# Queries in rows of four tokens: a new order of q, of the head pairs and of the factors in a retention and feed-forward kernel

## The chip, the cores and the metric

The kernel runs on one core of one Trainium2 chip. The metric is device time in microseconds. Of three runs of the kernel before, the median is 296.56 us (296.47 to 297.73). A profiled execution of its own gave the trace that is read here.

## The reference

Inputs are q, k and v of shape [8 batches, 8 heads, 576 tokens, 64], and two weights, w_in [512, 2048] and w_out [2048, 512], all fp32. Each head h has a decay gamma_h = 1 - 2^(-5-h):

```python
scores = scale * np.matmul(q, k.transpose(0, 1, 3, 2))        # scale = 1/8
Dmat = np.where(rel >= 0, gamma[:, None, None] ** rel, 0.0)   # rel = position of query - of key
ret = np.matmul(scores * Dmat, v)
x = ret.transpose(0, 2, 1, 3).reshape(4608, 512)
h = x @ w_in
g = h * np.tanh(softplus(h))
out = g @ w_out                                               # [4608, 512] fp32
```

## The kernel before

**Tiling.** The 4608 tokens are 36 chunks of 128. Chunks 0 to 7 are the first 128 tokens of each batch and have a code of their own at the start. Then come, for each pair of batches, chunks 1, 2 and 3 of either batch and one tail chunk (c = 4) that holds the last 64 tokens of both: 28 chunks, 24 of them whole (c < 4) and 4 tails. Four chunks make a tile t of 512 tokens; there are nine tiles.

**The dense part.** For a tile, `g1` (L579) multiplies w_in by xT, the transposed retention output, into a PSUM bank `hp` of 512 columns, and ScalarE (ACT) applies the activation (L590). `g2` (L595) multiplies by w_out into a bank `ops`; `store` (L640) copies it out and SyncE (SP) sends it to memory. All matmuls of both go through `product` (L551), which issues one of 512 columns (L553) or two of 256 (L558). There are two `hp` banks and one `ops` bank.

**The retention part.** The decay is split into a factor on the query and a factor on key and value: q is scaled by gamma^position, v by gamma^-position, and a causal mask of 64 by 64 is all that is left between them; keys stay unscaled. A running state (a sum of k times v over all earlier tokens of a batch) carries the rest. For chunk n the steps are:

- `load` (L298): on POOL's DMA queue, q, k and v of the chunk into `qkraw` and `vraw`, token by token, in pieces of 64 floats. Tiles `qkraw` have five buffers, `vraw` seven. Loads 12 and 13 are paced by hand: each waits for the landing of the sixth DMA before it (`paced`, L292).
- `step_p` (L322): on VectorE (DVE), two multiplications (L330) turn `qkraw` into `qks` in bf16, q with its factor `gq` and k with ones, and put the heads in pairs.
- `step_v` (L333): v times its factor, on DVE up to chunk 19 and on GpSimd (POOL) from chunk 20.
- `step_t` (L342): the eight 128x128 blocks of `qks` are transposed to `qkT`, up to chunk 13 on TensorE (PE, L351) with a copy by ACT, from chunk 14 by a DMA of SP (L359).
- `visit` (L524), once for every two chunks, 14 in all. It puts the attention matmuls of 64 by 64 on PE: the new states (`states`, L428), the outputs of the masked scores (`outputs`, L487), the queries times the state (`outputs_end`, L504), and the next two chunks' scores (`step_s`, L373). `outputs_copy` (L516) then copies the two banks of outputs, one by ACT and one by DVE, into `xT`, and `step_m` (L379) applies the mask.

The order of the work on each engine is written out by hand: loops over units of dense work call the steps at fixed units (L753 and L800), and every engine and queue works in that order. Each load on POOL's queue waits for the landing of the eighth DMA before it.

**The start.** DVE makes positions (`pos`, L135), distances (L151 to L153), the decay mask `dmask` (L156) and an identity (L158), then `ex` (L661, eight operations of 128x5) from which ACT makes the factors `gq` and `gv` (L662, L663), and casts the first q (L665). TensorE keeps warm with zeros (L170, L173), transposes the first chunks (L203) and makes their scores (L222) and outputs (L254).

Of the kernel before, what the change touches and what calls it, by code (L numbers as in the profile page):

```python
# [16 lines left out]
def kernel(  # L17
# [117 lines left out]
        nc.vector.memset(pos[:, c:c + 1], float(P * c))  # L135
    nc.vector.memset(pos[64:P, 4:5], 512.0 - 64.0)
    minus_p = consts.tile([P, 1], F32)
    late = consts.tile([P, P], F32)
    for i in (1, 0):
        for b in (2, 3):  # L140
# [6 lines left out]
    for f0 in (512, 768):  # L147
        load_w_in(f0, 256)
    mask = consts.tile([P, 64], F32)
    lg = [math.log(1.0 - 2.0 ** (-5.0 - h)) for h in range(H)]  # L150
    nc.vector.tensor_copy(minus_p, dist[:, 0:1])  # L151
    nc.vector.tensor_scalar(late, dist, 0.0, 1.0e6, op0=OP.is_lt, op1=OP.mult)
    nc.vector.tensor_tensor(dist, dist, late, op=OP.max)  # L153
# [3 lines left out]
    ex = consts.tile([P, 5, H], F32)  # L157
    nc.vector.tensor_scalar(ident, dist, 0.0, None, op0=OP.is_equal)  # L158

    nc.vector.tensor_scalar(pos, pos, minus_p, None, op0=OP.subtract)  # L160
# [126 lines left out]

    issued = []  # L290

    def paced(ins, n):  # L292

        if N0 + 3 < n < N0 + 6:
            behind(ins, issued[-6])
        issued.append(ins)

    def load(n, gate=None):  # L298
        if n >= n_chunks:
            return  # L300
        b, c = chunks[n]
        qkr = io.tile([P, 2, H, D], F32, name="qkraw")
        vr = io.tile([P, H, D], F32, name="vraw", bufs=7)
        live[n] = {"qkr": qkr, "v": vr}
        for t, src in ((qkr[:, 0], q), (qkr[:, 1], k), (vr, v)):
            if c < 4:
                ins = nc.gpsimd.dma_start(  # L307
                    out=t, in_=src[b, :, ds(P * c, P), :].rearrange("h p d -> p h d"))
                paced(ins, n)
                if gate is not None:  # L310
                    behind(ins, gate)
                    gate = None
            else:
                for e in range(2):
                    ins = nc.gpsimd.dma_start(
                        out=t[ds(64 * e, 64)],
                        in_=src[b + e, :, ds(512, 64), :].rearrange("h p d -> p h d"))
                    if gate is not None:
                        behind(ins, gate)
                        gate = None  # L320

    def step_p(n):  # L322
        c = chunks[n][1]
        qks = io.tile([P, 2, H, D], BF16, name="qks", bufs=4)
        live[n]["qks"] = qks
        slots = qks.rearrange("p i (g x y) d -> p (i g) y x d", x=2, y=2)
        heads = live[n]["qkr"].rearrange("p i (g y x) d -> p (i g) y x d", x=2, y=2)
        factors = gqk[:, c].rearrange("p i (g y x) -> p (i g) y x", x=2, y=2)
# [13 lines left out]
    def step_t(n, gate=None):  # L342
# [66 lines left out]
    def states(n):  # L409

        if n >= n_chunks:
            return [], 0
        st = ps_sc.tile([P, 2, 2, NP, 64], F32, name="sc")
        whole = [b for b, c in chunks[n:n + 2] if c == 1]
        s0 = ps_st.tile([P, 2, NP, 64], F32, name="st")[:, 0] if whole else None

        made = []

        def part(x, j, p):
            r = ds(64 * j, 64)  # L420
            for e in range(2):
                hh = 4 * (p // 2) + 2 * e + p % 2
# [12 lines left out]
        def unit(i, seen=None):  # L435
            made.clear()
            for p in range(NP):
                part(first_half[i], 0, p)
                part(second_half[i], 1, p)
            if seen is not None:  # L440
                behind(made[0], seen)
            return made[-4:]

        def sum_up():
            new = tr.tile([P, 5, NP, 64], F32, name="total", bufs=2)
            lows = tr.tile([P, 5, NP, 64], BF16, name="ssb", bufs=2)
# [32 lines left out]
    def outputs(n, banks):  # L479

        both = [pool.tile([P, NP, 2, 64], F32, name=name) for pool, name in banks]
        for x in range(2):
            vs = live[n + x]["vs"]
            for h in range(NP):
                for j in range(2):
                    for a in range(2):
                        nc.tensor.matmul(both[j][ds(64 * a, 64), h, x, :], lhsT=vs[ds(64 * j, 64), 2 * h + a, :],  # L487
                                         rhs=live[n]["sm"][ds(64 * j, 64), h % 2, x, 2 * (h // 2) + a, :],
                                         start=(x == 0 and h == 0), stop=False, skip_group_check=True)
        return both  # L490

    def outputs_end(n, both, other, seen=None):

        made = []
        for x in range(2):
            b, c = chunks[n + x]
            qk = live[n + x]["qk"]
            for g in range(2):
                for e in range(2):
                    j = e ^ other  # L500
                    state = st_sb[b, c, j] if c < 4 else st_sb[b + j, 4]
                    for a in range(2):
                        r, p = ds(64 * e, 64), 2 * g + a
                        made.append(nc.tensor.matmul(  # L504
                            both[j][ds(64 * a, 64), 2 * g + e, x, :], lhsT=state[r, p, :],
                            rhs=qk[r, 0, p, ds(64 * j, 64)], start=False, stop=True, skip_group_check=True))
# [4 lines left out]
    def outputs_copy(n, both, copies):  # L511
# [1 line left out]
        if s == 0:  # L513
            xts[t] = xp.tile([P, KC, NCH * P], BF16, name="xT")
        for j, copy in enumerate(copies):
            copy(xts[t][:, :, ds(P * s, 2 * P)].rearrange("p h (x j i) -> p j h x i", x=2, j=2)[:, j], both[j])  # L516

    held = consts.tile([P, 2], BF16)

# [137 lines left out]


    nc.scalar.activation(dmask, dmask, AX.Exp, bias=lnd[:, 0:1])
    for h in range(H):  # L660
        nc.vector.tensor_scalar(ex[:, :, h], pos, lg[h], None, op0=OP.mult)  # L661
    nc.scalar.activation(gq, ex, AX.Exp)  # L662
    nc.scalar.activation(gv, ex, AX.Exp, scale=-1.0)  # L663
    for b in range(2):
        dve(fst[0]["qb"][:, b, :], q0[:, b, :])  # L665
# [35 lines left out]
    nc.gpsimd.memset(mask, 1.0)  # L701
    for j in range(2):
        half = mask[ds(64 * j, 64)]
        nc.gpsimd.affine_select(out=half, in_=half, compare_op=OP.is_ge, fill=0.0,
                                base=0, pattern=[[1, 64]], channel_multiplier=-1)
    for b in range(4):
        load(N0 + b)
    nc.vector.tensor_scalar(gq, gq, 1.0 / math.sqrt(D), None, op0=OP.mult)
# [189 lines left out]
```

## Time and profile before

| | us |
|---|---|
| median of three runs | 296.56 (296.47 to 297.73) |
| the profiled execution's own time | 296.89 |
| its span, from the first to the last instruction | 295.2 |
| DVE, multiplications of q and k (L330) | 36.9 in 56 operations of 710 ns |
| POOL, issues of q's loads (L307) | 21.5 in 24 of 895 ns |
| PE, scores (L373), 448 matmuls 64x64x64 | 6.7 |
| copies of outputs to xT (L516), DVE and ACT | 9.0 (13 of 691 ns) and 8.2 (14 of 586 ns; one more stands by itself) |

How to read it: the first rows of the profile give each engine's busy time and its share of the span. The slices cut the span in 40 equal pieces; a digit is the busy share in tenths. The chain follows the work that ended last back from the end, and tells which engine held it up at each step. The timeline gives start, duration, engine, line, output and inputs of each instruction, "xN" for N merged ones, and in brackets how long the engine had been idle and for whom. The list of waits adds up who waited for whom. "L330" is line 330 of the kernel.

### The profile page before, as it was taken

To read this page: it belongs to the slowest core of one execution; us is meant where nothing else is said; L and a number is where in the kernel's file an instruction comes from. 1 tells how busy PE (TensorE), PEld (TensorE's weight loads), DVE (VectorE), ACT (ScalarE), POOL (GpSimd) and SP (SyncE) were. 2 spreads that over 40 slices of the span, in tenths; PEclk is the share of its full clock that TensorE was granted. 3 is DMA by queue.
4 is the path that set the end of the run, shared out by engine and by line. 5 is a ranking of instruction groups with operands and counts; after the bars stand their busy time and mean duration, and the time that the engine had idled before them with its cause. 6 is when DMAs were issued, how large, how long until landed. Compare 5 with 4: busy or idle time off the path is not lost.

```text
span 295.2 us, 7937 instructions
## 1 busy us (share of the span) xinstructions
PE 289.8 (98%) x3486; PEld 159.5 (54%) x3486; DVE 140.7 (48%) x252; ACT 128.2 (43%) x210; POOL 124.8 (42%) x163
## 2 busy tenths in 40 slices
PE   8999999999999999999999999999999999999995
PEld 5566887555557454547545454545454544444443
DVE  5861647589954829454645454535453321000011
ACT  4856226776545534443444434343435333333200
POOL 8845655487157295645576737292020000000000
PEclk9999999999999999999999999999999999999999
DMA  7999999999999999998979889686323111011122
GB/s 155 223 202 205 205 240 231 336 207 204 235 207 223 206 164 236 209 199 171 223 188 210 205 191 223 137 202 145 71 63 75 38 38 67 7 36 50 59 71 71
DMA packets 44067, 47.45 MB, mean 161 GB/s; under 512 B 25984, under 2 KB 33152, under 8 KB 44032
## 3 DMA queue, kind: packets, MB, share of 16 engines
q0 software_dynamic: 15120, 31.20, 50.5%
q1 hardware_dynamic: 28768, 15.54, 24.2%
q8 instruction: 27, 0.44, 0.6%
q10 hardware_dynamic: 144, 0.20, 0.2%
q14 instruction: 8, 0.07, 0.1%
HBM read 37.75 MB, written 9.44 MB: 160 GB/s over the span
## 4 chain that ended last, share of the span: by engine, by line
PE 94%; DMA 3%; POOL 2%; DVE 0%; issue 0%; POOLq 0%
PE hp L553 42%; PE ops L553 31%; PE hp L558 6%; PE ops L558 4%; DMA gT<-in_v_dram 3%; PE sc L373 1%; PE sc L428 1%; PE hp L504 1%; PE hp L487 1%; PE hp L634 1%; POOL gT L107 1%; PE st L558 1%; PE st L428 1%; PE sc L351 1%; PE sc L200 1%; POOL gT L118 0%
## 5 line engine op out<-in xcount | busy, mean ns | idle before, releaser
L553 PE MATMUL hp<-xT,w_in_t 128*128 128x512 bf16 (+1 forms) x524 | 128.2, 376 | 0.0
L590 ACT ACTIVATE gT<-hp 128x512 bf16<-128x512 f32 x142 | 84.7, 597 | 95.2 <-PE hp L553 94.2
L553 PE MATMUL ops<-w_out_t,gT 128*128 128x512 bf16 x416 | 102.6, 379 | 0.0
L553 PEld LDWEIGHTS <-w_in_t 128*128 128x128 bf16 x527 | 51.3, 98 | 53.9 <-issue 0.4
L553 PEld LDWEIGHTS <-gT 128*128 128x128 bf16 x470 | 44.7, 98 | 51.3
L642 DVE COPY res<-ops 128x512 f32<-128x512 f32 x28 | 19.3, 690 | 85.2 <-PE ops L553 85.2
L330 DVE TENSOR_TENSOR qks<-qkraw,gqk 128x512 bf16<-128x512 f32 x56 | 36.9, 710 | 3.6 <-DMA qkraw<-in_k_dram 3.3
L307 POOL DMA_DIRECT2D qkraw<-in_q_dram x24 | 21.5, 895 | 20.8 <-DVE qks L330 7.8
L516 DVE CAST xT<-hp 128x512 bf16<-128x512 f32 x13 | 9.0, 691 | 30.4 <-PE hp L504 30.4
L337 POOL TENSOR_TENSOR vs<-vraw,gv 128x512 bf16<-128x512 f32 x16 | 16.8, 1072 | 15.7 <-PE hp L487 15.6
L307 POOL DMA_DIRECT2D qkraw<-in_k_dram x24 | 21.3, 889 | 3.3 <-DMA vpair<-in_v_dram 1.5
L307 POOL DMA_DIRECT2D vraw<-in_v_dram x24 | 21.2, 884 | 1.8 <-DMA w_out_t<-in_moe_w_out_dram 1.0
L516 ACT CAST xT<-hp 128x512 bf16<-128x512 f32 x14 | 8.2, 586 | 28.6 <-PE hp L504 28.6
L558 PEld LDWEIGHTS <-gT 128*128 128x128 bf16 x180 | 17.3, 98 | 3.7
L522 POOL COPY held<-qkT 128x1 bf16<-128x1 bf16 x8 | 1.5, 187 | 37.7 <-DMA qkT<-qks 37.7
L464 DVE TENSOR_TENSOR total<-sc,total 128x256 f32<-128x256 f32 x40 | 16.9, 422 | 1.0
L379 DVE TENSOR_TENSOR sm<-sc,mask 128x1024 bf16<-128x1024 f32 x14 | 17.0, 1215 | 0.7 <-PE sc L373 0.7
L558 PE MATMUL hp<-xT,w_in_t 128*128 128x256 bf16 x104 | 15.9, 272 | 0.0
L558 PEld LDWEIGHTS <-w_in_t 128*128 128x128 bf16 x106 | 10.4, 98 | 6.6 <-issue 0.2
L467 ACT CAST ssb<-total 128x768 bf16<-128x768 f32 (+3 forms) x13 | 11.6, 895 | 3.3 <-DVE total L464 3.2
L553 PE MATMUL hp<-w_out_t,gT 128*128 128x512 bf16 x52 | 12.7, 379 | 0.0
L558 PE MATMUL ops<-w_out_t,gT 128*128 128x256 bf16 x96 | 12.4, 273 | 0.0
(134 smaller groups left out, 244.9 us busy)
## 6 DMA issues: line engine op xcount, KB each, us to landing
out_dram<-res SPq DMA_DIRECT2D x31, 256.0 KB, 3.6
qkraw<-in_q_dram POOLq DMA_DIRECT2D x24, 256.0 KB, 6.0
qkraw<-in_k_dram POOLq DMA_DIRECT2D x24, 256.0 KB, 6.4
vraw<-in_v_dram POOLq DMA_DIRECT2D x24, 256.0 KB, 6.7
w_out_t<-in_moe_w_out_dram POOLq DMA_DIRECT2D x4, 512.0 KB, 12.0
gT<-in_k_dram POOLq DMA_DIRECT2D x8, 128.0 KB, 6.5
gT<-in_v_dram POOLq DMA_DIRECT2D x2, 512.0 KB, 7.3
w_in_t<-in_moe_w_in_dram POOLq DMA_DIRECT2D x2, 512.0 KB, 10.9
```

Source lines behind the costliest of these rows:

```text
L307: ins = nc.gpsimd.dma_start(out=t, in_=src[b, :, ds(P * c, P), :].rearrange("h p d -> p h d"))
L330: nc.vector.tensor_tensor(slots[:, :, y], heads[:, :, y], factors[:, :, y].unsqueeze(3).to_broadcast([P, NP, 2, D]), op=OP.mult)
L337: engine.tensor_tensor(vs, live[n]["v"], gv[:, c, :].unsqueeze(2).to_broadcast([P, H, D]), op=OP.mult)
L379: nc.vector.tensor_tensor(sm.rearrange("p e x n i -> p (e x n) i"), live[n]["sc"].rearrange("p e x n i -> p (e x n) i"), mask.unsqueeze(1) ...
L428: ins = nc.tensor.matmul(to, lhsT=ks, rhs=vs, start=(x is not None or j == 0 and p == 0), stop=True, skip_group_check=True)
L464: nc.vector.tensor_tensor(new[:, k], st[:, j, x], total[b], op=OP.add)
L467: casts.append(lambda copy: copy(lows[:, 0:k], new[:, 0:k]))
L516: copy(xts[t][:, :, ds(P * s, 2 * P)].rearrange("p h (x j i) -> p j h x i", x=2, j=2)[:, j], both[j])
L553: newest[0] = nc.tensor.matmul(to, lhsT=w, rhs=x, start=first, stop=last)
L558: nc.tensor.matmul(to[:, ts(j, n)], lhsT=w, rhs=x[:, ts(j, n)], start=False, stop=False, skip_group_check=True)
L590: done = nc.scalar.activation(gts[t][:, f, :], hp, AX.Mish)
L642: copy(ot, ops)
```

## The change

For the 24 whole chunks, q is loaded in rows of four consecutive tokens (1 KB): partition 32p + g holds tokens 4g to 4g + 3 of a head, heads 0 to 3 in one DMA and 4 to 7 in a second. After the transposes the queries of a chunk so lie in the order (r, head, g), where the token is 4g + r; `queries` picks the 64 of a head and a half chunk as four runs of 16. Scores, mask and outputs keep that order of queries, and `outputs_copy` puts the tokens back in order as it writes `xT`. The four tail chunks load q as before and are read with steps of four columns. Heads are paired as h and h + 4 instead of within groups of four, in `qks`, in the states and in the outputs. The factors of q become a table `gq` by (r, half of the heads) with the positions of the new order, set up with 36 small memsets and seven operations; k gets no factor and is copied with a cast. The pacing of loads 12 and 13 goes.

```diff
+    lgs = consts.tile([P, H], F32)
+    for h in range(H):
+        nc.vector.memset(lgs[:, h:h + 1], lg[h])
+    lgp = consts.tile([P, 2], F32)
+    quarter = consts.tile([P, 1], F32)
+    for p in range(NP):
+        rows = ds(32 * p, 32)
+        nc.vector.memset(quarter[rows], -128.0 * p)
+        for x in range(2):
+            nc.vector.memset(lgp[rows, x:x + 1], lg[4 * x + p])
+    starts = consts.tile([P, 4, 4], F32)
+    for c in range(4):
+        for r in range(4):
+            nc.vector.memset(starts[:, c, r:r + 1], float(P * c + r))
...
+    nc.vector.tensor_scalar(group, minus_p, -4.0, quarter, op0=OP.mult, op1=OP.add)
+    nc.vector.tensor_scalar(posq, starts, group, None, op0=OP.add)
...
-    gqk = consts.tile([P, 5, 2, H], F32)
-    nc.vector.memset(gqk, 1.0)
-    gq = gqk[:, :, 0, :]
+    gq = consts.tile([P, 5, 4, 2], F32)
+    for x in range(2):
+        nc.vector.tensor_scalar(gq[:, 0:4, :, x], posq, lgp[:, x:x + 1], None, op0=OP.mult)
...
-        if N0 + 3 < n < N0 + 6:
-            behind(ins, issued[-6])
...
+        if c < 4:
+            for x in range(2):
+                moves.append((qr[:, ds(4 * x, 4), :], q[b, ds(4 * x, 4), ds(P * c, P), :].rearrange(
+                    "h (g r) d -> h g (r d)", r=4)))
...
-        for y in range(2):
-            nc.vector.tensor_tensor(slots[:, :, y], heads[:, :, y],
-                                    factors[:, :, y].unsqueeze(3).to_broadcast([P, NP, 2, D]), op=OP.mult)
+        if c < 4:
+            nc.vector.tensor_tensor(
+                qks[:, 0].rearrange("p (r x) d -> p r x d", x=2),
+                live[n]["qr"].rearrange("p (x r) d -> p r x d", r=4),
+                gq[:, c].unsqueeze(3).to_broadcast([P, 4, 2, D]), op=OP.mult)
...
+        nc.vector.tensor_copy(qks[:, 1].rearrange("p (n x) d -> p n x d", x=2),
+                              live[n]["kr"].rearrange("p (x n) d -> p n x d", x=2))
...
+    def queries(n, e, p, j):
+
+        qT = live[n]["qk"][ds(64 * e, 64), 0]
+        if chunks[n][1] == 4:
+            return qT[:, p, ds(64 * j, 64)].rearrange("d (g r) -> d r g", r=4)
+        return qT.rearrange("d r (p j g) -> d r p j g", j=2, g=16)[:, :, p, j, :]
...
-                        nc.tensor.matmul(sc[i, e, x, p, :], lhsT=qk[r, 1, p, i], rhs=qk[r, 0, p, i],
+                        nc.tensor.matmul(sc[i, e, x, p, :], lhsT=qk[r, 1, p, i], rhs=queries(n + x, e, p, j),
...
-                            both[j][ds(64 * a, 64), 2 * g + e, x, :], lhsT=state[r, p, :],
-                            rhs=qk[r, 0, p, ds(64 * j, 64)], start=False, stop=True, skip_group_check=True))
+                            both[j][ds(64 * a, 64), 2 * e + g, x, :], lhsT=state[r, p, :],
+                            rhs=queries(n + x, e, p, j), start=False, stop=True, skip_group_check=True))
...
-            copy(xts[t][:, :, ds(P * s, 2 * P)].rearrange("p h (x j i) -> p j h x i", x=2, j=2)[:, j], both[j])
+            copy(xts[t][:, :, ds(P * s, 2 * P)].rearrange("p h (x j g r) -> p j h x r g", x=2, j=2, r=4)[:, j],
+                 both[j].rearrange("p h x (r g) -> p h x r g", r=4))
...
-    for h in range(H):
-        nc.vector.tensor_scalar(ex[:, :, h], pos, lg[h], None, op0=OP.mult)
-    nc.scalar.activation(gq, ex, AX.Exp)
+    nc.vector.tensor_tensor(ex, pos.unsqueeze(2).to_broadcast([P, 5, H]),
+                            lgs.unsqueeze(1).to_broadcast([P, 5, H]), op=OP.mult)
+    nc.vector.tensor_copy(gq[:, 4].rearrange("p r x -> p (r x)"), ex[:, 4, :])
+    nc.scalar.activation(gq, gq, AX.Exp)
...
-                                base=0, pattern=[[1, 64]], channel_multiplier=-1)
+                                base=0, pattern=[[1, 4], [4, 16]], channel_multiplier=-1)
```

More of the change, by code (lines that the diff above doesn't have):

```diff
@@ L137 @@
     minus_p = consts.tile([P, 1], F32)
+    lg = [math.log(1.0 - 2.0 ** (-5.0 - h)) for h in range(H)]
+    lgs = consts.tile([P, H], F32)
[12 more added lines that the diff above has]
+            nc.vector.memset(starts[:, c, r:r + 1], float(P * c + r))
     late = consts.tile([P, P], F32)
@@ L149 @@
     mask = consts.tile([P, 64], F32)
-    lg = [math.log(1.0 - 2.0 ** (-5.0 - h)) for h in range(H)]
     nc.vector.tensor_copy(minus_p, dist[:, 0:1])
@@ L158 @@
     nc.vector.tensor_scalar(ident, dist, 0.0, None, op0=OP.is_equal)
+    group = consts.tile([P, 1], F32)
+    nc.vector.tensor_scalar(group, minus_p, -4.0, quarter, op0=OP.mult, op1=OP.add)
+    posq = consts.tile([P, 4, 4], F32)
+    nc.vector.tensor_scalar(posq, starts, group, None, op0=OP.add)
     nc.vector.tensor_scalar(pos, pos, minus_p, None, op0=OP.subtract)
-    gqk = consts.tile([P, 5, 2, H], F32)
-    nc.vector.memset(gqk, 1.0)
-    gq = gqk[:, :, 0, :]
+    gq = consts.tile([P, 5, 4, 2], F32)
+    for x in range(2):
+        nc.vector.tensor_scalar(gq[:, 0:4, :, x], posq, lgp[:, x:x + 1], None, op0=OP.mult)
     gv = consts.tile([P, 5, H], F32)
@@ L286, in cast_k0 @@
         nc.vector.tensor_tensor(k0[b], k0r[b], gv[:, 0, :].unsqueeze(2).to_broadcast([P, H, D]), op=OP.mult)
-    issued = []
-    def paced(ins, n):
-        if N0 + 3 < n < N0 + 6:
-            behind(ins, issued[-6])
-        issued.append(ins)
     def load(n, gate=None):
@@ L301, in load @@
         b, c = chunks[n]
-        qkr = io.tile([P, 2, H, D], F32, name="qkraw")
+        qr = io.tile([P, H, D], F32, name="qraw")
+        kr = io.tile([P, H, D], F32, name="kraw")
         vr = io.tile([P, H, D], F32, name="vraw", bufs=7)
-        live[n] = {"qkr": qkr, "v": vr}
-        for t, src in ((qkr[:, 0], q), (qkr[:, 1], k), (vr, v)):
-            if c < 4:
[L307 to L312, printed above, removed]
+        live[n] = {"qr": qr, "kr": kr, "v": vr}
+        moves = []
+        if c < 4:
+            for x in range(2):
+                moves.append((qr[:, ds(4 * x, 4), :], q[b, ds(4 * x, 4), ds(P * c, P), :].rearrange(
+                    "h (g r) d -> h g (r d)", r=4)))
+        for t, src in ((qr, q), (kr, k), (vr, v))[c < 4:]:
+            if c < 4:
+                moves.append((t, src[b, :, ds(P * c, P), :].rearrange("h p d -> p h d")))
             else:
                 for e in range(2):
[L315 to L320, printed above, removed]
+                    moves.append((t[ds(64 * e, 64)], src[b + e, :, ds(512, 64), :].rearrange("h p d -> p h d")))
+        for to, src in moves:
+            ins = nc.gpsimd.dma_start(out=to, in_=src)
+            if gate is not None:
+                behind(ins, gate)
+                gate = None
     def step_p(n):
@@ L325, in step_p @@
         live[n]["qks"] = qks
-        slots = qks.rearrange("p i (g x y) d -> p (i g) y x d", x=2, y=2)
-        heads = live[n]["qkr"].rearrange("p i (g y x) d -> p (i g) y x d", x=2, y=2)
-        factors = gqk[:, c].rearrange("p i (g y x) -> p (i g) y x", x=2, y=2)
-        for y in range(2):
-            nc.vector.tensor_tensor(slots[:, :, y], heads[:, :, y],
-                                    factors[:, :, y].unsqueeze(3).to_broadcast([P, NP, 2, D]), op=OP.mult)
+        if c < 4:
[3 more added lines that the diff above has]
+                gq[:, c].unsqueeze(3).to_broadcast([P, 4, 2, D]), op=OP.mult)
+        else:
+            nc.vector.tensor_tensor(
+                qks[:, 0].rearrange("p (n x) d -> p n x d", x=2),
+                live[n]["qr"].rearrange("p (x n) d -> p n x d", x=2),
+                gq[:, c].rearrange("p r x -> p (r x)").rearrange("p (x n) -> p n x", x=2).unsqueeze(3)
+                .to_broadcast([P, NP, 2, D]), op=OP.mult)
+        nc.vector.tensor_copy(qks[:, 1].rearrange("p (n x) d -> p n x d", x=2),
+                              live[n]["kr"].rearrange("p (x n) d -> p n x d", x=2))
     def step_v(n):
@@ L421, in part @@
             for e in range(2):
-                hh = 4 * (p // 2) + 2 * e + p % 2
+                hh = 4 * e + p
                 if x is None:
@@ L487, in outputs @@
                         nc.tensor.matmul(both[j][ds(64 * a, 64), h, x, :], lhsT=vs[ds(64 * j, 64), 2 * h + a, :],
-                                         rhs=live[n]["sm"][ds(64 * j, 64), h % 2, x, 2 * (h // 2) + a, :],
+                                         rhs=live[n]["sm"][ds(64 * j, 64), h // 2, x, 2 * (h % 2) + a, :],
                                          start=(x == 0 and h == 0), stop=False, skip_group_check=True)
@@ L496, in outputs_end @@
             b, c = chunks[n + x]
-            qk = live[n + x]["qk"]
             for g in range(2):
@@ L703 @@
         half = mask[ds(64 * j, 64)]
-        nc.gpsimd.affine_select(out=half, in_=half, compare_op=OP.is_ge, fill=0.0,
-                                base=0, pattern=[[1, 64]], channel_multiplier=-1)
+        nc.gpsimd.affine_select(out=half.rearrange("p (r g) -> p r g", r=4), in_=half.rearrange("p (r g) -> p r g", r=4), compare_op=OP.is_ge, fill=0.0,
+                                base=0, pattern=[[1, 4], [4, 16]], channel_multiplier=-1)
     for b in range(4):
```

## The prediction

> **What bounds the kernel now.** I read the page's busy times and slices first, then its chain, then the chain and the timeline in narrow windows. The page:
>
> ```profile
> PE 289.8 (98%) x3486; PEld 159.5 (54%) x3486; DVE 140.7 (48%) x252; ACT 128.2 (43%) x210; POOL 124.8 (42%) x163
> ...
> PE   8999999999999999999999999999999999999995
> ...
> PEclk9999999999999999999999999999999999999999
> DMA  7999999999999999998979889686323111011122
> ...
> PE 94%; DMA 3%; POOL 2%; DVE 0%; issue 0%; POOLq 0%
> ```
>
> TensorE is busy in every slice at the full granted clock and is 94% of the chain; DVE, ACT and POOL are under half busy. The DMA engines are full for the first half, yet only 3% of the chain is DMA. That 3% lies at the start (chain of the first 17 us):
>
> ```profile
> 6.14 8.11 DMA gT<-in_v_dram
> 14.26 0.02 issue
> 14.28 0.71 DVE vb L236 x2
> ...
> 15.56 0.98 PE hp L565 x8
> ```
>
> The first values land at 14.26, are cast, and the dense matmuls run from 15.56 to the end. From there the chain is PE pieces one behind the other: 256-column matmuls at 109 ns (chain: 14 in 1.53 us, L558), nowhere an idle row over a few hundred ns. So the time is a start of 15.5 us, set by DMA, and a gapless PE stream. A change gains only by shortening one of the two, and loses wherever it opens a hole in the stream.
>
> **Part 1: q's loads (L307, 24 chunks).** Removed: one DMA of 256 KB in pieces of 256 B, 895 ns to issue on POOL. Added: two of 128 KB in rows of 1 KB. The nearest issue rows are L107 (128 rows each, 530 to 566 ns) and L315 (half a chunk, 694 ns): 1.1 to 1.4 us for the two, so POOL pays 0.2 to 0.5 us more a chunk, 5 to 12 us in all on an engine busy 124.8 of 295.2 us. Cover: in the DMA-bound stretch (34 to 48 us run at about 208 GB/s, one 256 KB load per 1.25 us) POOL waits for landings anyway, since each load waits for the landing of the eighth DMA before it (the list of waits: POOL qkraw <- DMA vpair 3.4 us, though vpair has nothing to do with qkraw). Later POOL idles by several us between visits (POOL held <- DMA qkT 37.7 us in all). Two slots of eight per q instead of one leave two chunks in flight instead of 2.7, still over 6 us of transfers.
>
> The transfer itself: between no gain and the page's best slice (336 GB/s, 0.78 us instead of 1.25), 0 to 0.47 us a chunk. I take half; it is worth nothing at the end, as no PE row waits for it. The pacing that goes (loads 12 and 13 wait for the sixth DMA before; one POOL wait of 2.9 us) lets these loads start earlier: also nothing on PE.
>
> **Part 2: the factors (L330, 28 chunks).** Two DVE multiplies of 128x512 fp32 to bf16, 0.60 us start to start, 1.28 us a chunk, become one multiply (0.68) and one plain cast of k. The same cast stands in L236 (DVE, 128x512 bf16<-f32, 427 ns). So about 1.0 us a chunk, 0.25 to 0.3 saved, 7 to 8 us of DVE. DVE waits 85 us for PE at the stores alone, so nearly all of it is idle time. One place shows PE waiting for this line:
>
> ```profile
> 69.92 0.86 PE ops L553 x4
> 70.78 0.03 issue
> 70.81 0.62 PE sc L351 x8
> ```
>
> Eight transposes take 0.45 us elsewhere (chain, 50.54) and 0.62 here; DVE's L330 ended at 70.75. With the step 0.25 us shorter the 0.2 us go: **-0.2 us**.
>
> **Part 3: queries as strided operands (L373 and L504, 448 matmuls each).** The counts stay; the moving operand becomes four runs of 16 columns, 256 B apart, in place of 64 in a row (steps of 8 B in the four tail chunks). No row has a strided moving operand. Per visit the three pieces concerned take 0.14, 0.32 and 0.17 us (chain at 124.99, 125.12, 125.44). Lower end: nothing. Upper end: columns at half rate; 64 columns are 27 ns (109 x 64/256), four matmuls run side by side on the quarters of the array, 16 such sets a visit, 14 visits: 16 x 14 x 27 ns = 6.0 us. A gain is excluded, as the column count stays. I take nothing: each run of 16 is itself contiguous. [...]
>
> **Part 4: the copies to xT (L516, 15 on ACT, 13 on DVE).** They now write 2-byte elements 8 B apart. After a visit, timeline:
>
> ```profile
> 125.30 0.32 PE L504 MATMUL hp<-qkT,ssb 64*64 64x64 bf16 x16
> ...
> 125.55 1.04 PE L553 MATMUL ops<-w_out_t,gT 128*128 128x512 bf16 x4
> 125.65 0.69 DVE L516 CAST xT<-hp 128x512 bf16<-128x512 f32 x1 [1.49 <-PE hp L504]
> 125.70 0.58 ACT L516 CAST xT<-hp 128x512 bf16<-128x512 f32 x1 [2.31 <-PE hp L504]
> ...
> 126.42 1.89 PE L553 MATMUL hp<-xT,w_in_t 128*128 128x512 bf16 x8
> ```
>
> Both copies empty the two hp banks. Four output matmuls cover them for 0.87 us; then PE wants the first bank, ACT's, at 126.42. ACT is done at 126.28: **cover 0.14 us**. DVE's bank is wanted 0.86 us later, cover 0.9. Nearest rows: L208 writes runs of 8 B with gaps of 8 B and reads PSUM at steps of 256 B, in 588 ns on ACT and 691 on DVE, against 585 to 589 and 690 for contiguous copies of the size. Striding cost nothing there, so I take nothing. Upper end: half rate, +0.42 us on ACT (128x1024 takes 1012 ns, 128x512 588), less the cover, 14 times: 3.9 us.
>
> **Part 5: set-up on DVE.** 36 one-column memsets come in front of L151, which now waits until 2.95 for POOL's dist:
>
> ```profile
> 1.16 0.09 DVE L135 MEMSET pos<- 128x1 f32 x5
> 1.32 0.06 DVE L136 MEMSET pos<- 64x1 f32 x1
> 2.95 0.15 DVE L151 COPY minus_p<-dist 128x1 f32<-128x1 f32 x1 [1.57 <-POOL dist L130]
> ...
> 5.14 1.04 DVE L661 TENSOR_SCALAR ex<-pos 128x5 f32<-128x5 f32 x8
> 5.72 1.05 DVE L665 CAST gT<-gT 128x512 bf16<-128x512 f32 x2
> ```
>
> The memsets have 1.57 us of idle time. At the pace of L135 (9 ns each) they fit; at that of the small L661 (72 ns) they take 2.6 us; five changes of partition group at 0.12 us (L135 to L136) add 0.6. So L151 is 0 to 1.6 us late (2.6 + 0.6 - 1.57); at POOL's pace for the same memsets (four from 0.31 to 0.41, 33 ns) 1.2 + 0.6 us, late by 0.25. I take that. Behind ident, ten operations (L160, L162, eight L661: 0.83 us) become seven, three of them waiting for the one in front (0.25 us, as L152 to L153; the rest at 72 ns): about 1 us, 0.2 more. A delay reaches the end only past the slack: the k transposes hold PE from 6.61 to 7.08 while the casts end at 6.77 (0.3), and DVE waits 0.23 us at 14.28 for v. 0.25 + 0.2 is just inside 0.5: nothing; upper end 1.3 us. A gain is excluded, since v's landing stays.
>
> The heads' new pairs, the mask (L704, two of 235 ns) and the outputs' rows change places within the same tiles and counts: nothing.
>
> **Sum.** -0.2 +0 +0 +0 against the profiled execution's own 296.89 us (span 295.2 and 1.7 around it): 296.7. The median of the runs shown, 296.56, lies 0.3 below that execution; taken from it, **296.4 us**. About 0.5% (1.5 us) is what a measurement of this kernel can tell from no change.
>
> **Rivals.**
> *Slower, by the copies to xT.* Place: the first L553 into hp behind each visit. It decides from an ACT copy of 0.58 + 0.14 = 0.72 us. At half rate 3.9 us, 300.5 us. For it: the cover is thin, and no row writes single 2-byte elements with gaps. Against: the L208 rows. Chance 0.10.
> *Slower, by the strided operand.* At half rate +6.0, 302.4 us. Against it: whole runs of 32 B. Chance 0.06.
> [...] Chance 0.06. [...]
> *The change does what it says for DMA and DVE, and nothing follows*: this is my forecast, as both are off the path. Chance 0.65, own range 295.6 to 297.7 (no gain to the memsets' 1.3 us, and the spread of the runs).
> *Faster by over 1.5 us*: would need PE's stream or v's landing to shorten, for which I find 0.2 us. Chance 0.07. What remains, 0.06, is a hole that this trace does not show, by POOL's dearer issues or k's cast beside POOL.
>
> **Numbers.** Faster 0.07, within 0.5% 0.65, slower 0.10 + 0.06 + 0.06 + 0.06 = 0.28. The range runs from 295.6 over the copies' and the loads' cases to 300.6; it leaves out faster (0.07), the strided operand beyond that (0.06) and about half of the unseen.
>
> **What would show it.** Part 1: q's landings no later than now, POOL 5 to 12 us busier. Part 2: DVE down by 7 us, the piece at 70.8 back at 0.45. Part 3: 32 L373 in 0.32 us. Part 4: ACT's L516 at 586 ns, the L553 behind four output matmuls without idle. Part 5: L151's counterpart before 3.3, vb at 14.28. Wrong if L516 passes 0.72 us, if a score piece lengthens, or if L351's counterpart waits for q.

## The result, and the profile after

The changed kernel takes **304.06 us** (median of six executions, 304.02 to 304.40), the kernel before on the same chip 297.05 (six, 296.47 to 298.06): ratio 1.0234, 95% interval 1.0214 to 1.0255. The prediction, 296.4 with a range to 300.6, was wrong. Ratios leave out executions far above a kernel's fastest; where the executions of an experiment spread, all of them are told.

The profiled execution took 304.4 us, its span 302.7 (295.2 before). From its page, busy times, PE's slices and the chain's shares:

```profile
PE 291.5 (96%) x3486; PEld 159.7 (53%) x3486; DVE 140.7 (46%) x285; ACT 138.5 (46%) x210; POOL 140.3 (46%) x187
...
PE   6899999999999999999999999999999999999995
...
PE 90%; ACT 5%; DVE 3%; issue 1%; POOL 1%; POOLq 0%; ACTq 0%
```

PE still shows 9 in every slice but the first two and the last, since a hole of half a microsecond doesn't show in a slice of 7.6 us. The chain tells more: ACT, absent before, now has 5%. DVE is as busy as before, 140.7, though its multiplications became cheaper, so something else on it became dearer. The groups name it (busy us, mean ns of one, idle before):

```profile
L578 PE MATMUL hp<-xT,w_in_t 128*128 128x512 bf16 (+1 forms) x524 | 128.2, 376 | 4.7 <-ACT xT L540 4.7
...
L540 ACT CAST xT<-hp 128x512 bf16<-128x512 f32 x14 | 18.2, 1299 | 28.6 <-PE hp L528 28.6
L540 DVE CAST xT<-hp 128x512 bf16<-128x512 f32 x13 | 16.8, 1292 | 36.1 <-PE hp L528 36.1
```

L540 is L516 of before, the copies to xT: 1.29 us each on both engines, where they took 0.585 and 0.691. And PE, which had waited for none of these copies, now waits for ACT's, 4.7 us by this list. The timeline behind a visit shows how (start, duration):

```profile
112.22 1.29 DVE L540 CAST xT<-hp 128x512 bf16<-128x512 f32 x1 [3.05 <-PE hp L528]
...
112.23 1.04 PE L578 MATMUL ops<-w_out_t,gT 128*128 128x512 bf16 x4
112.26 1.29 ACT L540 CAST xT<-hp 128x512 bf16<-128x512 f32 x1 [2.44 <-PE hp L528]
...
113.60 1.67 PE L578 MATMUL hp<-xT,w_in_t 128*128 128x512 bf16 x7 [0.33 <-ACT xT L540]
```

The four output matmuls are issued within 0.87 us of 112.23; the next wants ACT's bank, which is empty at 113.55, and starts at 113.60. From one matmul's start to the next, less the usual 0.22 us, such a hole is 0.46 to 0.64 us, 6.6 us in 12 of 14 visits. The difference of 7.5 us between the spans of the two profiled executions is, from their traces:

| place | us |
|---|---|
| holes behind 12 visits | +6.6 |
| one hole at 78.2, for which the profile names no wait ("issue") | +0.35 |
| matmuls with queries: tail chunks (steps of 8 B) +0.33, the rest (runs of 16) +0.09 | +0.4 |
| dense part begins at 15.95 instead of 15.56 | +0.4 |
| transposes at 71 us | -0.2 |

### The profile page after: what moved, and what is told of

It reads as the page before. It is cut to its first block, busy times and chain, and to the rows that moved or that the text cites. A ratio compares the mean times of both kernels' runs of the same rounds, so it can differ in the third digit from the quotient of the medians.

```text
span 302.7 us, 8012 instructions
## 1 busy us (share of the span) xinstructions
PE 291.5 (96%) x3486; PEld 159.7 (53%) x3486; DVE 140.7 (46%) x285; ACT 138.5 (46%) x210; POOL 140.3 (46%) x187
## 4 chain that ended last, share of the span: by engine, by line
PE 90%; ACT 5%; DVE 3%; issue 1%; POOL 1%; POOLq 0%; ACTq 0%
PE hp L578 41%; PE ops L578 27%; PE hp L583 6%; ACT xT L540 5%; PE ops L583 3%; PE hp L528 2%; PE sc L398 1%; PE hp L512 1%; PE hp L659 1%; PE sc L453 1%; PE st L583 1%; DVE sm L244 1%; PE st L453 1%; PE sc L218 1%; PE sc L369 1%
## 5 line engine op out<-in xcount | busy, mean ns | idle before, releaser
L328 POOL DMA_DIRECT2D qraw<-in_q_dram x56 | 40.6, 727 | 22.9 <-PE ops L578 10.2
L540 DVE CAST xT<-hp 128x512 bf16<-128x512 f32 x13 | 16.8, 1292 | 36.1 <-PE hp L528 36.1
L540 ACT CAST xT<-hp 128x512 bf16<-128x512 f32 x14 | 18.2, 1299 | 28.6 <-PE hp L528 28.6
L328 POOL DMA_DIRECT2D kraw<-in_k_dram x32 | 28.1, 879 | 2.8 <-DMA kraw<-in_k_dram 2.0
L328 POOL DMA_DIRECT2D vraw<-in_v_dram x32 | 28.0, 876 | 2.6 <-DMA vpair<-in_v_dram 2.6
L338 DVE TENSOR_TENSOR qks<-qraw,gq 128x512 bf16<-128x512 f32 x24 | 16.4, 682 | 0.2 <-DMA qraw<-in_q_dram 0.2
L348 DVE CAST qks<-kraw 128x512 bf16<-128x512 f32 x28 | 12.9, 461 | 1.6 <-DMA kraw<-in_k_dram 1.6
```

What stands on the lines that cost most here:

```text
L328: ins = nc.gpsimd.dma_start(out=to, in_=src)
L338: nc.vector.tensor_tensor(qks[:, 0].rearrange("p (r x) d -> p r x d", x=2), live[n]["qr"].rearrange("p (x r) d -> p r x d", r=4), gq[:, c] ...
L348: nc.vector.tensor_copy(qks[:, 1].rearrange("p (n x) d -> p n x d", x=2), live[n]["kr"].rearrange("p (x n) d -> p n x d", x=2))
L540: copy(xts[t][:, :, ds(P * s, 2 * P)].rearrange("p h (x j g r) -> p j h x r g", x=2, j=2, r=4)[:, j], both[j].rearrange("p h x (r g) -> p ...
```

## The experiments

The first theory is that the copies' strided writes are the whole loss but for the start. Its rival is that the loss lies in several parts, q's loads among them.

### The copies alone, and the steps

**e2**: the kernel before, its copies to xT with the change's writes and nothing else. The tokens come out in another order.

```diff
-            copy(xts[t][:, :, ds(P * s, 2 * P)].rearrange("p h (x j i) -> p j h x i", x=2, j=2)[:, j], both[j])
+            copy(xts[t][:, :, ds(P * s, 2 * P)].rearrange("p h (x j g r) -> p j h x r g", x=2, j=2, r=4)[:, j],
+                 both[j].rearrange("p h x (r g) -> p h x r g", r=4))
```

> The kernel before, with nothing changed but the copies to xT, which write 8 B apart as in the changed kernel (the tokens of each half chunk so come out in another order; nothing else differs). Theory: L516 at 1.3 us on both engines and 297.05 + 6.6 = 303.6 us, some 6.5 of the 7 us that the whole change cost. Rival (the loads, the strided queries or the set-up carry the loss): under 300 us.

Measured: 303.98 us (303.31 to 304.57), ratio 1.0228 (1.0206 to 1.0251). Its groups show the same wait:

```profile
L554 PE MATMUL hp<-xT,w_in_t 128*128 128x512 bf16 (+1 forms) x524 | 128.1, 376 | 4.8 <-ACT xT L516 4.8
```

By the medians the writes alone cost 6.85 us, the whole change 7.0. The smaller places of the table above are lost in the spread of the runs.

**e3**: the kernel before with another pattern of writes or reads at each visit, and fp32 stores in steps in three tiles; kind "w" writes every r-th element, kind "r" reads PSUM in steps and writes in a row. Tokens come out in other orders.

```diff
...
+            if kind == "w":
+                copy(to.rearrange("p h x (g r) -> p h x r g", r=r), both[j].rearrange("p h x (r g) -> p h x r g", r=r))
+            elif kind == "r":
+                copy(to.rearrange("p h x (g r) -> p h x g r", r=r), both[j].rearrange("p h x (r g) -> p h x g r", r=r))
...
```

> The kernel before with another access pattern in the copies of each visit (outputs in another order, times of single copies are what is read): writes of bf16 at steps of 2, 4, 8 and 16 elements, reads of PSUM at steps of 2, 4 and 16, runs of 2 and 4 elements, and two visits where one engine strides and the other does not; and fp32 stores at steps of 2, 4 and 8 elements. Theory (each write that leaves the 4-byte word or the line costs extra): writes at a step of 2 (4 B) about 0.6 to 0.9 us, at 4 about 1.3, at 8 and more 1.3 or above; reads at any step 0.59 and 0.69; runs of 4 with gaps as contiguous; one engine striding alone still 1.3 us. Rival (the two engines hinder each other): an engine that strides alone takes clearly less than 1.3 us. Rival (reordering as such costs): reads slow too.

Measured, one execution of 301.26 us, durations from the timeline:

| 512 columns, PSUM fp32 to SBUF bf16 | ACT us | DVE us |
|---|---|---|
| in a row | 0.585 | 0.691 |
| every 2nd element (4 B) | 0.730 | 0.732 |
| every 4th (8 B), the change | 1.29 | 1.29 |
| every 8th (16 B) | 2.41 | 2.41 |
| every 16th (32 B) | 2.32 | 2.32 |
| PSUM read in steps of 2, 4 or 16, written in a row | 0.585 | 0.691 |
| two copies of 256, in a row | 0.37, 0.38 | 0.42, 0.41 |
| two of 256, pairs of elements 16 B apart | 0.38, 0.39 | 0.42, 0.41 |
| two of 256, runs of four 16 or 32 B apart | 0.37, 0.38 | 0.42, 0.41 |

Stores of 512 fp32 elements by DVE take 0.69 us at steps of 8 B and 1.07 at 16 and 32. So the lone 2-byte element is the dear one: 16 B apart it takes 4.7 ns, a lone 4-byte element 2.1. Two 2-byte neighbours, one 4-byte word, cost nothing more even 16 B apart (0.38 and 0.42 us for 256 columns, 0.37 and 0.42 in a row), and stepping through PSUM is free (0.585 and 0.691 us). Two visits had one strided copy each. In the first it is ACT's:

```profile
129.37 0.69 DVE L530 CAST xT<-hp 128x512 bf16<-128x512 f32 x1 [1.49 <-PE hp L507]
129.41 1.30 ACT L522 CAST xT<-hp 128x512 bf16<-128x512 f32 x1 [2.31 <-PE hp L507]
...
130.76 0.59 PE L567 MATMUL hp<-xT,w_in_t 128*128 128x512 bf16 x2 [0.46 <-ACT xT L522]
```

In the second DVE's copy took 1.30 us, ACT's 0.59, and PE had no hole. A copy that strides alone takes the same 1.30 us, so the two engines aren't in each other's way; and only ACT's bank decides.

**e1**: the changed kernel with the order mended on the reading side.

```diff
-            copy(xts[t][:, :, ds(P * s, 2 * P)].rearrange("p h (x j g r) -> p j h x r g", x=2, j=2, r=4)[:, j],
-                 both[j].rearrange("p h x (r g) -> p h x r g", r=4))
+            copy(xts[t][:, :, ds(P * s, 2 * P)].rearrange("p h (x j g r) -> p j h x g r", x=2, j=2, r=4)[:, j],
+                 both[j].rearrange("p h x (r g) -> p h x g r", r=4))
```

> The changed kernel, but the copies to xT put the tokens in order as they read PSUM (steps of 64 B) and write rows without gaps. Theory (it is the writes of 2-byte elements 8 B apart that cost): L540 back from 1.30 to 0.59 us on ACT and 0.69 on DVE, the holes behind the visits (0.46 to 0.64 us, 12 of them, 6.6 us) gone, 304.06 - 6.6 = 297.4 us. Rival (any reordering in these copies costs, whichever side): L540 stays near 1.3 us and the time at 304. Rival (the strided queries, the loads of q or the dearer POOL issues carry part of the 7 us): L540 recovers, but the time stays above 298.5.

Measured: the copies are back at 0.586 and 0.692, the holes are gone, but the twelve executions spread from 297.44 to 303.6, median 299.34 (ratio 1.0062, 1.0030 to 1.0094). The profiled one, 303.1, near the top of the spread, has a wait that the kernel before hasn't, in the list of waits (us, times, longest) and in the chain that leads to 144 us:

```profile
PE sc L398 <- DMA qkT<-qks: 3.7, 1, 3.7
```

```profile
129.25 15.22 DMA qkT<-qks
```

A DMA transpose lands 15.2 us after its issue; the longest was 8.1 in the kernel before and 7.5 in the changed one. The first theory therefore isn't all: with the copies mended, a second loss shows.

The wait costs more than its own 3.7 us. Just behind it, from 145.8 to 149.2 us, TensorE's granted clock is 0.50 instead of 1.00, and its matmuls of 512 columns start 0.43 us apart instead of 0.22. Half of these 3.4 us is lost: 3.7 + 1.7 = 5.4, of the 5.7 us between this execution and the fastest of e1.

**e4**: e1 with the query factors' set-up issued behind the first casts (group, pos, posq, ex: `set_up(0)`) and the first transposes (gq and gv: `set_up(1)`).

```diff
...
+    set_up(0)
     keep_warm(4, long=4)
...
     f_transpose(0, 1, 1, [(ps_h, "hp", act), (ps_h, "hp", act)])
+    set_up(1)
...
```

> As e1, and the set-up of the query factors on DVE moved behind the casts of the first q and behind the first transposes. Theory (the 0.4 us that the changed kernel's dense part starts later come from the set-up operations ahead of those casts, two of which sat for 0.8 us until a DMA issue of POOL ended): the dense part starts at 15.6 us instead of 15.95, and the time is 0.3 to 0.4 us below e1, near 297.0. Rival (the memsets in front, which stay where they are, cost it): no difference from e1.

Measured: dense part from 15.41 us instead of 15.95, so the 0.4 us are the set-up's. Twelve executions from 296.89 to 303.47, median 297.93 (ratio 1.0020, 0.9992 to 1.0049). The spread stays.

### q's loads

**e5**: the kernel before with the change's `load` alone.

```diff
...
+            for x in range(2):
+                moves.append((qr[:, ds(4 * x, 4), :], q[b, ds(4 * x, 4), ds(P * c, P), :].rearrange(
+                    "h (g r) d -> h g (r d)", r=4)))
...
```

> The kernel before with the changed kernel's load() alone: q of 24 chunks in two halves of 128 KB, rows of four tokens, and the pacing of loads 12 and 13 gone; all else as before, so q's tokens and heads stand in other places and the output is another one. In the two earlier kernels that read PSUM in steps, the executions lay between 296.9 and 303.6 us, and in the profiled ones the scores waited once for a DMA transpose of q and k (landing 15.2 and 14.3 us after issue; at most 8.1 in the kernel before): 3.8 and 3.0 us of TensorE. Theory A, the new q loads make these transposes late: the same spread here, some executions about 297, others 300 to 304, median 298 to 300. Theory B, something else of the change does it (strided operands, the shorter multiply, other places of the copies): 296.5 to 298.5 like the kernel before, no wait for a transpose.

Measured: **319.38 us** (315.47 to 321.7), ratio 1.0699 (1.0648 to 1.0750), far worse than any theory had it. Transposes land up to 16.7 us after issue, and the scores wait 13.1 us for them in four places. The clock falls here too, as the page's slices show:

```profile
PE   8899999999894499999589999999999999999995
...
PEclk9999999999999589999969999999999999999999
```

It is 0.50 from 102.1 to 112.3 and from 156.7 to 163.5 us; PE is busy for 9.1 us of that and so loses 4.6. With 2.1 us in which PE waits for ACT, the sum is 19.8 of the 20.6 us between this execution, 317.95, and the median before. Such stretches stand in the traces of e1, e4, e5, e10, e11 and e15, each behind a wait of PE of 2.5 us or more. In the traces without such a wait the clock, where it is recorded, doesn't fall before the last 2 us.

**e6**: e4 with the `load` of before.

> The changed kernel with PSUM read in steps, the set-up behind the first casts, and the load() of the kernel before (q in one DMA of 256 B pieces, loads 12 and 13 paced); q's tokens then stand in other rows than the rest takes them for, and the output is another one. Theory A, the new q loads make the transposes late: 296.5 to 298 in every execution, no transpose over about 8 us from issue to landing. Theory B, another part does it: executions from 297 to 303 as with the new loads, a score waiting 3 to 4 us for a transpose in some.

Measured: 296.93 us (296.89 to 297.19, eleven executions), ratio 0.9989 (0.9979 to 0.9998). The rest of the change is harmless, and the spread is q's loads. The `load` of before brings its pacing back as well; e8 below shows that the pacing is worth nothing.

**e7**: e4 with the 32 groups in front of the four heads.

```diff
...
-                    "h (g r) d -> h g (r d)", r=4)))
+                    "h (g r) d -> g h (r d)", r=4)))
...
-        return qT.rearrange("d r (p j g) -> d r p j g", j=2, g=16)[:, :, p, j, :]
+        return qT.rearrange("d r (j g p) -> d r p j g", j=2, g=16)[:, :, p, j, :]
...
```

> The changed kernel with PSUM read in steps, the set-up behind the first casts, and q's halves loaded with the 32 groups of four tokens as the first dimension and the four heads behind them (partition 4g + h instead of 32h + g; the factors and the queries follow). Bytes, rows of 1 KB and the number of DMAs stay. Theory A1, the first dimension of four heads puts a half on few DMA engines and the transposes wait behind it: here the spread goes, 296.5 to 298 in every execution. Theory A2, it is the number of DMAs, the 1 KB rows or the missing pacing: the spread stays, 297 to 303, with transposes that land 10 to 15 us after issue. If two heads' rows of one partition step by 147 KB cost more in the transfer itself, q's loads land later than 5.5 us (median) and the median rises by up to 1 us.

Measured: 301.87 us (301.55 to 302.26), ratio 1.0154 (1.0139 to 1.0170). Neither theory's time. The late transposes are gone, none over 6.2 us, and POOL issues one of q's loads in 593 ns instead of 717. But the queries now lie 8 B apart in all chunks, and PE pays. Its chain in a visit:

```profile
126.70 0.24 PE hp L541 x16
126.94 0.48 PE sc L411 x31
127.42 0.24 PE hp L541 x16
```

The same pieces take 0.13, 0.40 and 0.13 us in e6; by the matmuls' starts L411 and L541 take 4.4 us more in all, of the 4.9 between the two medians.

**e8**: the kernel before without `paced`.

> The kernel before without the pacing of loads 12 and 13, which the change takes away too; nothing else. Theory A1 and A2 but for the pacing: 296.5 to 298.5, as before, transposes land within about 8 us. Theory C, the pacing alone kept the loads from piling up in front of the transposes: executions from 297 to 303, with a score waiting 3 us or more for a transpose.

Measured: 297.66 us (296.86 to 298.35), ratio 1.0008 (0.9994 to 1.0022). The pacing is nothing.

### Where the tiles lie

Why did these loads cost 22 us in e5 and, it seemed, 0 to 6 in e1? In e5 and the kernel before, a 4096-byte packet of the loads takes some 310 ns; in e6 it takes 195, and in e1, e4 and the changed kernel half of them take under 230. These programs differ in where their tiles begin in a partition, by the sizes of the constants in front (each reckoned as rounded up to 32 B, the author's assumption, which no trace shows; e13 below, moved by 96 B, fits it). The change drops a table of 320 B and adds seven of together 416: everything behind moves by 96 B. Reckoned from the tiles' sizes, the loads' first tile so goes from 160 B behind a multiple of 256 to a multiple. No trace holds addresses; the steps between the places follow from the edits. An unused tile moves it at will, 8 numbers by 32 B (e9 and e13 move the kernel before, e10 and e14 e5, e11 and e15 the changed kernel), 24 by 96, 32 by 128:

```diff
     minus_p = consts.tile([P, 1], F32)
+    pad = consts.tile([P, 8], F32)
```

> The kernel before with one unused constant tile of 32 bytes a partition in front of its other tiles; no instruction differs. In the kernel before every tile of the loads begins 32 bytes behind a multiple of 64 in its partition; here all begin at a multiple, as they do in the changed kernel, whose constants are 96 bytes larger. Theory A, the place decides the DMA packets' time: the 4096-byte packets of q, k and v, of which half take over 300 ns before (mean 308 ns from 40 to 50 us), take about 195 ns here; the transposes land in 2.7 to 5 us; TensorE, gapless already, gives 296.5 to 297.3, little spread. Theory B, it is q and k in two tiles instead of one that made the packets short: 308 ns and 297.0 to 297.5 as before.

> The kernel before with the changed kernel's load() alone (q in two halves in rows of four tokens, 319.4 us), moved by the same 32 bytes to multiples of 64; the output is that of other tokens' places, as there. Theory A, the new loads and the place of the tiles add up: far from 319, at 297 to 304 in a spread as the changed kernel had it with PSUM read in steps (299.3 median), since that one has these loads at multiples of 64. Theory B, the 319 come from q and k in one tile: 315 to 321 again.

> The changed kernel with the unused tile of 32 bytes: its tiles then begin 32 bytes behind a multiple of 64, as in the kernel before. No instruction differs. Theory A, the change moved the tiles by chance, and that hid the price of its q loads: 310 to 326 (304.1 and some or all of the 22 us that the loads cost in the kernel before), scores waiting for transposes that land 10 us and more after issue. Theory B, the place is nothing: 304.0 to 304.4.

Measured: e9 297.57 us, ratio 1.0010 (0.9995 to 1.0025), packets 308 ns as before. e10 329.54 us (318.95 to 333.52). e11 **334.21 us** (331.65 to 337.9), ratio 1.1217 (1.1166 to 1.1268), with no instruction changed. Both lie above what either theory gave. Multiples of 64, which e9 and e10 had, help nothing: that part of theory A fell. That the place counts was borne out by e11. All short packets so far belonged to multiples of 256, so:

> The kernel before with an unused tile of 96 bytes a partition in front: its tiles then begin at multiples of 256, as they do in the changed kernel and in every kernel so far whose 4096-byte packets took 195 ns; 32, 64, 96 and 160 bytes behind a multiple all gave 300 ns and more. No instruction differs. Theory A2 (the place counts, but by multiples of 128 or 256, not of 64): 195 ns from 40 to 50 us, transposes landing in 2.7 to 5 us, 296.4 to 297.2 us. Theory B (q and k in two tiles): 308 ns as before, 296.5 to 298.3.

> The kernel before with the changed kernel's load() alone, as in the runs of 319 and 330 us, and its tiles at multiples of 256; the output is that of other tokens' places. Theory A2: 297 to 304 in a spread, transposes up to 15 us in the stretch from 110 to 150 us, no more. Theory B: 315 us and more, as with the tiles 32 or 64 bytes off.

> The changed kernel with an unused tile of 128 bytes: its tiles begin 128 bytes behind a multiple of 256. No instruction differs. If multiples of 128 are enough: 304.0 to 304.4 and packets of 195 ns. If it takes multiples of 256: packets of 300 ns, 315 us and more, as 32 bytes off gave 334.

Measured: e13 296.62 us (296.15 to 296.94), ratio 0.9979 (0.9969 to 0.9989). e14 298.22 (296.27 to 301.93, ten executions). e15 315.09 (311.85 to 317.66), ratio 1.0535 (1.0497 to 1.0572). Theory A2 held in all three, and 128 is not enough. What e13 gains lies nearly all at the start: in its trace the dense part begins at 14.99 us instead of 15.56. The transfers from 40 to 46 us, when nothing but loads runs, of the kernel before and of e13 (packets, MB, mean rate):

```profile
DMA packets 382, 1.32 MB, mean 219 GB/s; under 512 B 61, under 2 KB 61, under 8 KB 382
```

```profile
DMA packets 616, 2.06 MB, mean 343 GB/s; under 512 B 114, under 2 KB 114, under 8 KB 616
```

The same kind of loads, all engines full both times (their packets' time is 103.4% and 103.1% of the 16 engines' window), and 1.57 times the bytes. A 4096-byte packet takes some 310 and 195 ns. Why a place off a multiple of 256 B costs this isn't shown.

The same window tells what the new q loads do at a good place. This is e14, which differs from e13 in `load` alone:

```profile
DMA packets 845, 1.44 MB, mean 240 GB/s; under 512 B 495, under 2 KB 495, under 8 KB 845
```

The engines are as full (105.0%), and yet they move 240 GB/s instead of 343 (244 in the changed kernel). So the new loads are slower, though their rows are longer.

| us | tiles off multiples of 256 | at multiples |
|---|---|---|
| before | 297.2 (160 B, measured with e13), 297.57 (192) | 296.62 |
| before with the new q loads | 319.38 (160), 329.54 (192) | 298.22 |
| the change | 334.21 (32), 315.09 (128) | 304.06 |

How the off-place loads stop the change can be read in the waits of e11:

```profile
PE sc L399 <- DMA qkT<-qks: 23.5, 3, 11.4
...
DVE qks L339 <- DMA qraw<-in_q_dram: 15.4, 5, 8.9
```

Half clock behind these waits adds some 4.8 us in this trace (9.6 us of PE's work).

### What is worth keeping

**e12**: pairs h and h+4, one multiplication for q and a cast for k; q's loads, the order of tokens, the set-up and the copies as before. Its tiles lie at multiples of 256.

> The part of the change that costs nothing, without the rows of four tokens: head pairs h and h+4, one multiply for q and a cast for k; q's loads, the order of the tokens, the set-up, the paced loads and the copies as before. Its tiles begin at multiples of 64. If the change's loss is all in the rows of four (strided writes, q's loads, set-up) and the shorter multiply is worth its 0.2 us at the transposes of 70 us: 296.3 to 297.0, ratio 0.997 to 1.000 to before, little spread. If the pairs or the cast beside POOL cost something unseen: over 297.5.

Measured: **296.28 us** (296.03 to 296.67, twelve executions), ratio 0.9973 (0.9961 to 0.9985). That is 0.3% under the kernel before, with the interval clear of 1. But e13 has 0.9979 (0.9969 to 0.9989) without any part of the change, so the place of the tiles is enough to explain it; that the pairs and the cast add anything isn't shown.

## Why the prediction was wrong

- **Part 4, the step that failed.** "Striding cost nothing there, so I take nothing": the row it leaned on, L208, writes runs of four elements, which e3 finds free (0.37 to 0.38 and 0.41 to 0.42 us for 256 columns, as in a row); the change writes single ones, which cost 2.2 times on ACT. The nearest row was near in step and far in what decides. The rival had the place and the threshold right (ACT's copy past 0.72 us, first matmul into hp). Its price was too small: half rate, +0.42 us, where +0.71 was measured. By its own sum, 0.71 less 0.14 of cover, times 12 visits, is 6.8 us; 6.6 came. It had a chance of 0.10, and its 300.5 (296.4 + 3.9 is 300.3) stood at the end of the range.
- **One step, three prices.** The prediction took nothing for the strided operand and for the strided writes alike. At steps of 8 B, e3's fp32 stores by DVE were free (0.69 us; 1.07 at 16 B), its single bf16 elements took 1.29 us, and PE's moving operand paid too, 4.4 us in all in e7. The length of the step alone doesn't tell the price.
- **Part 5, small but wrong.** The memsets fitted (L151's counterpart starts at 2.94). What came late is the arithmetic behind ident:

```profile
4.93 2.35 POOL L118 DMA_DIRECT2D gT<-in_v_dram  x2
...
5.25 0.86 DVE L178 TENSOR_SCALAR pos<-pos,minus_p 128x5 f32<-128x5 f32 x1
...
6.38 0.89 DVE L687 COPY gq<-ex 128x8 f32<-128x8 f32 x1
6.46 1.08 DVE L691 CAST gT<-gT 128x512 bf16<-128x512 f32 x1
```

  Two operations of 5 and 8 columns last 0.9 us. They end at 6.11 and 7.27, when POOL's two issues of v end (6.12 and 7.28). Operations of 16 and 40 columns beside the same issues took 0.23 and 0.20 us, so why these two were held stays open. The kernel before had one such hold: of its eight L661, shown in Part 5, the later six all end from 6.14 on, as POOL's first issue does. The prediction read a pace of 72 ns from them and priced seven operations at 1 us; with a second hold the first q casts ended at 7.87 instead of 6.77, past the slack of 0.5, and 0.4 us came out at the end, which e4 took back. (Against e13, which has its tiles at the same place and begins at 14.99, the set-up cost 1.0 us in these single traces, and e4 took back half.)
- **Part 1 looked right and wasn't.** In the changed kernel no row of PE waits for q, as foreseen. But POOL is 15.5 us busier against 5 to 12, and the transfers were priced between no gain and a gain, while at one place of the tiles the rate fell from 343 GB/s to 240. The changed kernel doesn't show it, because the change itself moved the tiles and so altered the measured rate of 208 GB/s from which this part was priced. The case of dear q loads (chance 0.06) was real. But the number of DMA engines that a load goes to, from which its place in the range was worked out, is shown by no run; the runs showed the price alone: 22 us in e5, up to 30 in e11, 0 to 6 at multiples of 256. That the copies' holes gave these loads time in the changed kernel is argued, not shown.
- **Why the new loads are slow stays argued.** e7 fits a cause in the first dimension of q's loads, four heads: with 32 groups in front no transpose is late (none over 6.2 us). Its constants put its tiles 96 B off a multiple, so a better place isn't the reason; off a multiple the loads move 236 GB/s in e7, 219 in the kernel before and 212 and 202 with the change's loads (e5, e11). But e7 also changes the partitions' order, and which engines carry what isn't in the trace, so the cause was not shown.
- **Part 3 was right** for runs of 16: +0.09 us. Rival 2 waits at the next corner: steps of 8 B cost 0.3 us in the four tail chunks and 4.4 us in e7, where its half rate in 14 visits gave 6.0.
- **Part 2 was right where it counted**: DVE's steps fell from 36.9 to 32.0 us (16.4 and 2.7 for q, 12.9 for k), 4.9 us instead of the 7 to 8 foreseen, and the chain has the foreseen piece:

```profile
71.18 0.45 PE sc L369 x8
```

## What to carry to other kernels

When a copy has to change the order of 2-byte elements, step on the PSUM side and write in a row (0.585 us on ACT here, against 1.29 for single elements 8 B apart), or move pairs (0.38 us for 256, as in a row); a strided row covers a new pattern only if its runs are as short. Before a DMA pattern is judged, look at where its tile begins in the partition: an unused tile of 96 B sped the old loads up by a factor of 1.6 here (219 to 343 GB/s), and one of 32 B cost the changed kernel 30 us. One loss can stand in front of another; mend the first and measure again. And a long wait of TensorE is dearer than it looks, since the granted clock was 0.50 behind every wait of 2.5 us or more here.

## What the runs showed of the hardware

- Loads in pieces of 256 B into tiles off a multiple of 256 B: 219 GB/s (160 B off in the kernel before, 192 in e9); at a multiple: 343 (e13). With the change's q loads: 240 at a multiple (e14), 212, 202 and 197 off one (160 B in e5, 32 in e11, 128 in e15); with e7's, 236 at 96 B off. All from 40 to 46 us; the places are reckoned.
- Single bf16 elements written 16 B apart: 4.7 ns each on ACT and on DVE, the same on both (2.41 us for 512), against 1.1 and 1.35 in a row; single fp32 elements by DVE 2.1 (e3).
- Two small DVE operations between buffers in SBUF, of 0.86 and 0.89 us, ended when the DMA issue of POOL beside them ended; two others took 0.23 and 0.20 us beside the same issues (the changed kernel).
- Behind waits of 2.5 us and more TensorE's granted clock was 0.50 for 3.4 to 20.4 us, part of which fell into the waits (e1, e4, e5, e10, e11, e15).
